# Experts' second layer: products of 256 columns in place of 512, in two passes over a token tile

## The chip, the core and the metric

The kernel runs on one core of one Trainium2 chip. Its engines work side by side and meet through semaphores: TensorE (PE in the profile, with its weight loads as PEld), VectorE (DVE), ScalarE (ACT), GpSimd (POOL) and SyncE (SP), which issues most of the transfers. The time is the device time of one execution in microseconds; before the change it was 1222.12 us, the median of three runs (1220.14 to 1223.38).

## What is computed

Three layers follow one another on 1152 tokens (2 x 576) of width 512, all in float32:

```
q_pool = q.reshape(B, H, S // 2, 2, D).mean(axis=3)                # attention on pooled queries
attn = softmax(scale * q_pool @ k^T);  x = attn @ v                # 2 x 8 heads, 1152 keys, width 64
h = x @ w_in;  x = (h * tanh(softplus(h))) @ w_out                 # 512 -> 2048 -> 512
P = exp(x @ w_gate - max), 8 rounds of row and column scaling       # the gate, 1152 x 8
for e in range(8):                                                  # experts, 512 -> 1024 -> 512
    h = np.maximum(x @ w1[e], 0.0)
    ye = h @ w2[e]
    out += P[:, e:e + 1] * ye
```

The change lies in `h @ w2[e]`, the experts' second layer.

## The kernel before

To keep float32 accuracy, every operand of a large product is split into a high and a low part of type fp32r, and a product is made as three: high weight x low data and the like (names end in h and l). Each product loads 128 x 128 values as weights and streams the other operand past them, up to 512 columns, into a bank of PSUM (128 x 512 float32 values). Eight banks are shared by the pools `ps_o` (three) and `ps_h` (five).

The experts are cut along their hidden width of 8 x 1024 into 64 chunks of 128. The first four chunks go ahead (called the shared layer here, group -1 in the code); the other 60 form 20 groups of three (`groups`, line 958). A group is worked off in two stages:

- first layer (`product`, line 1081): 15 block products in a scheme that saves products by adding blocks, each of 6 products of 384 columns, 90 in all. DVE and ACT combine the banks and write the hidden values, split, to `hhall` and `hlall`;
- second layer (`down`, line 1234): for each of the nine token tiles of 128 tokens, three chunks x three operand pairs, 9 products of 512 columns into one bank `po`; the hidden values are the weights of a product, the expert's matrix `wdb` streams past. When the last product is done, DVE multiplies the bank by the gate and adds it to `oacc` in one instruction (line 1259). Where a group crosses from one expert to the next (5 of 20 groups), a tile has two banks, one for each expert, and two such instructions (`segments`, line 961). The shared layer has 12 products a tile, and ACT copies the bank (line 1255).

In the last group the last tile of `TILES` (tile 3) is already made in two halves: `parts` is 2, and each half of 256 columns has a bank, an addition and an output transfer of its own.

The order of the work is written out by hand: each engine runs its instructions in the order in which the loops at lines 1289 to 1317 issue them. Between two tiles of the second layer `next_weights` prepares the next group's weights on DVE, ACT and POOL (`w_sum`, `w_split`, `down_split`). In the shared layer, group 0 and at the start of group 1, the gate's rounds are put between the tiles (`gate_step`): each is a small product on PE (`psk`, line 913), which reads `csum`, and a short chain on DVE that ends with the reduction to the next `csum` (lines 903 to 918).

Of the kernel before, what the change touches and what calls it, by code (L numbers as in the profile page):

```python
# [23 lines left out]
def pool_attention_mish_sinkhorn_kernel(  # L24
# [12 lines left out]
    nc = tc.nc  # L37
# [263 lines left out]
    with ExitStack() as actx:  # L301
# [234 lines left out]
        c0, c1 = 2 * P, SQ  # L536
# [264 lines left out]
    def hidden(c, a, b):  # L801
        return tuple((y if c == NFC - 1 else x[:, c, :])[:, a:b] for x, y in hall)
# [43 lines left out]
    while len(todo) > NDC or k < NB:  # L846
# [3 lines left out]
        while len(todo) > NDC and todo[0][0] <= k and room >= todo[0][1]:  # L850
            _, n, s, th, dc = todo.pop(0)
# [109 lines left out]
    def segments(g):  # L961

        if g < 0:
            return [(0, list(range(NFC)))]
        es = [c // NHC for c in groups[g]]
        return [(e, [j for j in range(CH) if es[j] == e]) for e in sorted(set(es))]
# [253 lines left out]
    def token_rows(t):  # L1220

        cuts = sorted({0, P} | {x - t * P for b in range(B) for x in range(b * SQ, (b + 1) * SQ + 1, P)
                                if 0 < x - t * P < P} | {x * SQ - t * P for x in range(B) if 0 < x * SQ - t * P < P})
        for a, z in zip(cuts, cuts[1:]):
            b, i = divmod(t * P + a, SQ)
            if i < MID * P:
                r = b * SQ + i % P * MID + i // P
                yield slice(a, z), slice(r, r + (z - a - 1) * MID + 1, MID)
            else:
                yield slice(a, z), slice(b * SQ + i, b * SQ + i + z - a)  # L1230
# [3 lines left out]
    def down(g, t):  # L1234

        end = g == NG - 1
        parts = 2 if end and t == TILES[-1] else 1
        w = DM // parts
        for si, (e, sl) in enumerate(segments(g)):
            gate = Pm[:, t, e:e + 1]  # L1240
            for j in range(parts):
                pl, tag = (ps_h, "h") if (3 <= t < 8 if g < 0 else si) else (ps_o, "o")
                ps = pl.tile([P, 512], F32, tag=tag, name=f"po{g}_{t}_{e}_{j}")
                cs = slice(j * w, (j + 1) * w)
                ops = []
                for c in sl:
                    hh, hl = hidden(c, t * P, (t + 1) * P)
                    whi, wlo = wdt[g, c]
                    ops += [(hh, wlo), (hl, whi), (hh, whi)]
                for n, (a, b) in enumerate(ops):  # L1250
                    nc.tensor.matmul(  # L1251
                        ps[:, 0:w], lhsT=a, rhs=b[:, cs], start=(n == 0), stop=(n == len(ops) - 1))
                oa = oacc[:, t, cs]
                if g < 0:
                    nc.scalar.activation(oa, ps[:, 0:w], AF.Copy)
                elif g == 0:
                    nc.vector.tensor_tensor(out=oa, in0=ps[:, 0:w], in1=oa, op=ALU.add)
                else:
                    nc.vector.scalar_tensor_tensor(  # L1259
                        out=oa, in0=ps[:, 0:w], scalar=gate, in1=oa, op0=ALU.mult, op1=ALU.add)  # L1260
                if end and e == segments(g)[-1][0]:
                    for rows, to in token_rows(t):
                        nc.sync.dma_start(out=out[to, cs], in_=oa[rows])
# [25 lines left out]
    for t in range(NTT):  # L1289
        down(-1, t)  # L1290
        next_weights(0, t - 2)
        if t == 7:
            gate_step()

    spare += [hp_.tile([P, 3, TH], F32, tag="last" + x, name="spare" + x) for x in "hl"]
    for g in range(NG):
        for k, n in enumerate(ORDER3):
            product(g, n)
            after(g, n)
            if k + NSL < NP:  # L1300
                w_split(g, k + NSL)
            if k in ((0, 7, 9) if g == 0 else (7, 9)):
                down_split(g, {0: 0, 7: 1, 9: 2}[k])
            if k == 9 and g + 1 < NG:
                raw_up(g + 1)
            if (g, k) in ((0, 0), (1, 0)):
                gate_step()
            if g == 1 and k in (10, 12, 14):
                assert not gate_steps
                scale(k // 2 - 5)  # L1310
        for k, t in enumerate(TILES):
            down(g, t)
            next_weights(g + 1, k)
            if g == 0 and k in (1, 3, 4, 6, 7):
                gate_step()
            if g == 1 and k + 3 < NTT:
                scale(k + 3)
# [30 lines left out]
```

## Time and profile before

| what | us |
|---|---|
| median of three timed runs | 1222.12 |
| the profiled execution | 1218.55 |
| its span, first to last instruction | 1215.9 |
| PE busy | 1200.9 (99%) |
| weight loads busy | 1108.4 (91%) |
| DVE / POOL / ACT busy | 851.1 / 656.2 / 592.3 |

The profile is of one execution. Products on PE overlap in it: the duration of one is longer than the distance from its start to the next start, so a pace is read from starts or from the chain, not from durations. The chain of waits follows the work that ended last back from the end; consecutive products of one line are merged into one piece of it with their number. Times in a timeline are microseconds from the start of the span.

### The profile page before, as it was taken

To read this page: it belongs to the slowest core of one execution; us is meant where nothing else is said; L and a number is where in the kernel's file an instruction comes from. 1 tells how busy PE (TensorE), PEld (TensorE's weight loads), DVE (VectorE), ACT (ScalarE), POOL (GpSimd) and SP (SyncE) were. 2 spreads that over 40 slices of the span, in tenths; PEclk is the share of its full clock that TensorE was granted. 3 is DMA by queue.
4 is the path that set the end of the run, shared out by engine and by line. 5 is a ranking of instruction groups with operands and counts; after the bars stand their busy time and mean duration, and the time that the engine had idled before them with its cause. 6 is when DMAs were issued, how large, how long until landed. Compare 5 with 4: busy or idle time off the path is not lost.

```text
span 1215.9 us, 19367 instructions
## 1 busy us (share of the span) xinstructions
PE 1200.9 (99%) x6840; PEld 1108.4 (91%) x6840; DVE 851.1 (70%) x1576; ACT 592.3 (49%) x1357; POOL 656.2 (54%) x758
## 2 busy tenths in 40 slices
PE   8999999999999999999999999999999999999998
PEld 7999999999999999888988889999888889999887
DVE  7889999965444334787866678776866677766865
ACT  7889999976544443543333223333332233333331
POOL 7567877425443332475655556645545566555551
PEclk9999999999999999999999999999999999999999
DMA  6788888644232210011101111111111111111112
GB/s 193 256 274 278 282 283 282 230 145 139 70 93 82 70 44 18 1 53 53 53 23 39 52 53 45 52 53 53 33 38 44 53 44 53 53 52 42 33 40 78
DMA packets 51984, 116.38 MB, mean 96 GB/s; under 512 B 7977, under 2 KB 22897, under 8 KB 51889
## 3 DMA queue, kind: packets, MB, share of 16 engines
q1 hardware_dynamic: 48400, 103.36, 26.1%
q0 software_dynamic: 3488, 11.80, 3.6%
q8 instruction: 54, 0.88, 0.3%
q14 instruction: 42, 0.34, 0.1%
HBM read 66.86 MB, written 2.40 MB: 57 GB/s over the span
## 4 chain that ended last, share of the span: by engine, by line
PE 91%; DVE 4%; DMA 2%; issue 1%; ACT 1%; SPq 0%; POOL 0%; ACTq 0%
PE po L1251 30%; PE c L1081 26%; PE ph L234 10%; PE po L820 8%; PE psS L484 5%; PE psA L585 5%; PE psT L564 3%; DMA er<-e 2%; DVE e L489 2%; DVE etl L570 1%; PE psk L419 1%; ACT e L503 0%; DMA kraw<-in_k_dram 0%; PE pg L875 0%; PE psq L462 0%
## 5 line engine op out<-in xcount | busy, mean ns | idle before, releaser
L82 POOL TENSOR_TENSOR wslotsl<-s,wslotsh 128x256 fp32r<-128x256 f32 x180 | 131.5, 739 | 238.0 <-ACT wslotsh L75 238.0
L1259 DVE SCALAR_TENSOR_TENSOR oacc<-po,Pm,oacc 128x512 f32<-128x512 f32 (+1 forms) x217 | 161.1, 746 | 102.4 <-PE po L1251 95.9
L1251 PE MATMUL po<-wdbl,hhall 128*128 128x512 f32 (+1 forms) x543 | 214.4, 395 | 0.0
L1251 PE MATMUL po<-wdbh,hlall 128*128 128x512 f32 (+1 forms) x543 | 214.1, 394 | 0.0
L1251 PE MATMUL po<-wdbh,hhall 128*128 128x512 f32 (+1 forms) x543 | 214.0, 394 | 0.0
L1098 ACT ACTIVATE t<-c 128x384 f32<-128x384 f32 x80 | 39.2, 489 | 247.3 <-PE c L1081 247.3
L1118 ACT ACTIVATE hhall<-c 128x384 fp32r<-128x384 f32 x180 | 88.5, 492 | 127.7 <-DVE c L1114 125.0
L1251 PEld LDWEIGHTS po<-wdbh,hhall 128*128 128x128 f32 x543 | 102.1, 188 | 24.3
L1251 PEld LDWEIGHTS po<-wdbl,hhall 128*128 128x128 f32 x543 | 102.1, 188 | 23.3
L1251 PEld LDWEIGHTS po<-wdbh,hlall 128*128 128x128 f32 x543 | 102.1, 188 | 23.2
L82 POOL TENSOR_TENSOR wslotsl<-rawu,wslotsh 128x256 fp32r<-128x256 f32 x120 | 91.0, 772 | 50.2 <-ACT wslotsh L75 50.2
L570 DVE TENSOR_TENSOR etl<-psT,eth 128x384 fp32r<-128x384 f32 (+1 forms) x240 | 108.2, 509 | 7.3 <-ACT eth L567 6.6
L489 DVE TENSOR_SCALAR_CACHE_REDUCE e<-psS 128x1152 f32<-128x1152 f32 x72 | 97.6, 1356 | 17.7 <-PE psS L484 13.8
L1119 DVE SCALAR_TENSOR_TENSOR hlall<-c,hhall 128x384 fp32r<-128x384 f32 x180 | 98.7, 548 | 2.0
L567 ACT ACTIVATE eth<-psT 128x384 fp32r<-128x384 f32 (+1 forms) x240 | 92.1, 472 | 6.9 <-PE psT L564 6.5
L1081 PE MATMUL c<-x2l,wslotsh 128*128 128x384 f32 x280 | 94.3, 337 | 0.0
L1081 PE MATMUL c<-x2h,wslotsl 128*128 128x384 f32 x280 | 94.2, 336 | 0.0
L1081 PE MATMUL c<-x2h,wslotsh 128*128 128x384 f32 x280 | 93.9, 335 | 0.0
L503 ACT ACTIVATE e<-e,nm 128x1152 f32<-128x1152 f32 x70 | 89.2, 1274 | 2.7 <-DVE e L489 1.8
L484 PE MATMUL psS<-kT,qT 128*128 128x384 f32 x384 | 81.9, 348 | 1.9 <-DVE e L489 1.5
L75 ACT ACTIVATE wslotsh<-s 128x256 fp32r<-128x256 f32 x180 | 72.0, 410 | 23.9 <-DVE s L1047 23.8
L585 PE MATMUL psA<-etl,vst 128*128 128x256 f32 (+1 forms) x288 | 81.2, 304 | 0.8 <-DVE rs L512 0.4
(368 smaller groups left out, 3065.0 us busy)
## 6 DMA issues: line engine op xcount, KB each, us to landing
er<-e SPq DMA_DIRECT2D x70, 576.0 KB, 4.1
rawd<-in_moe_w_dram SPq DMA_DIRECT2D x60, 256.0 KB, 2.8
rawu<-in_moe_w_dram SPq DMA_DIRECT2D x30, 384.0 KB, 3.3
raw<-in_moe_w_in_dram SPq DMA_DIRECT2D x16, 512.0 KB, 3.8
raw<-in_moe_w_out_dram SPq DMA_DIRECT2D x16, 512.0 KB, 3.7
vraw<-in_v_dram POOLq DMA_DIRECT2D x15, 288.0 KB, 4.3
kraw<-in_k_dram POOLq DMA_DIRECT2D x13, 288.0 KB, 4.1
qT<-qT SPq DMA_DIRECT2D x28, 128.0 KB, 4.8
```

The costliest lines, as they stand in the source:

```text
L82: eng.tensor_tensor(out=lo, in0=src, in1=hi.bitcast(F32), op=ALU.subtract)
L234: nc.tensor.matmul(ps[:, 0:TH], lhsT=a, rhs=b, start=(n == 0), stop=(n == len(ops) - 1))
L484: nc.tensor.matmul(ps[:, kb, 0:TH], lhsT=a, rhs=kt[:, kb * TH:(kb + 1) * TH], start=(n == 0), stop=(n == len(ops) - 1))
L489: nc.vector.tensor_scalar(sc, ps[:, :, 0:TH], -1.0, None, op0=ALU.mult, op1=ALU.min, accum_out=nm)
L567: nc.scalar.activation(eh[:, cs, o:o + b - a], ps[:, 0:3, a:b], AF.Copy)
L570: nc.vector.tensor_tensor(out=el[:, cs, o:o + b - a], in0=ps[:, 0:3, a:b], in1=eh[:, cs, o:o + b - a].bitcast(F32), op=ALU.subtract)
L585: nc.tensor.matmul(box["ps"][:, 0:n], lhsT=vst[p, j][:, c].rearrange("p a d -> p (a d)"), rhs=(el, eh)[which][:, c, 0:n], start=(c == 0 an ...
L820: nc.tensor.matmul(ps[:, 0:TH], lhsT=a, rhs=b, start=(n == 0), stop=(n == len(ops) - 1))
L1081: nc.tensor.matmul(cb[c], lhsT=a_, rhs=b_, start=FIRST[n] and m == 0, stop=LAST[n] and m == len(ops) - 1, skip_group_check=True)
L1119: los.append(lambda: nc.vector.scalar_tensor_tensor(out=lo, in0=b, scalar=0.0, in1=hi.bitcast(F32), op0=ALU.max, op1=ALU.subtract))
L1251: nc.tensor.matmul(ps[:, 0:w], lhsT=a, rhs=b[:, cs], start=(n == 0), stop=(n == len(ops) - 1))
L1259: nc.vector.scalar_tensor_tensor(out=oa, in0=ps[:, 0:w], scalar=gate, in1=oa, op0=ALU.mult, op1=ALU.add)
```

## The change

Only `down` changes. In place of one pass over the operand pairs with 512 columns, a loop over `c0` makes one whole pass for columns 0 to 255 and then one for 256 to 511. Both halves lie in the same bank; each begins its sum anew (`start`) and ends it (`stop`). So each weight block is loaded twice, once for each half. The tile's evacuation still reads the whole bank at once, after the second half. The last tile of the last group, with `w` = 256, is as before.

```diff
--- before.py
+++ after.py
@@ -1247,9 +1247,11 @@
                     hh, hl = hidden(c, t * P, (t + 1) * P)
                     whi, wlo = wdt[g, c]
                     ops += [(hh, wlo), (hl, whi), (hh, whi)]
-                for n, (a, b) in enumerate(ops):
-                    nc.tensor.matmul(
-                        ps[:, 0:w], lhsT=a, rhs=b[:, cs], start=(n == 0), stop=(n == len(ops) - 1))
+                for c0 in range(0, w, 256):
+                    for n, (a, b) in enumerate(ops):
+                        nc.tensor.matmul(
+                            ps[:, c0:c0 + 256], lhsT=a, rhs=b[:, cs.start + c0:cs.start + c0 + 256],
+                            start=(n == 0), stop=(n == len(ops) - 1))
                 oa = oacc[:, t, cs]
                 if g < 0:
                     nc.scalar.activation(oa, ps[:, 0:w], AF.Copy)
```

The order of the instructions on DVE, ACT, POOL and SP is the same in both kernels, with the same waits. On PE there are 1719 rows more. Two places show it. The first is a token tile of the last group (`po_5_7_0`: tile 5, expert 7), with the row ahead of it and the first one of the last tile. Before:

```order
L1251 MATMUL po_4_7_0_12745<-wdbh,hhall 128x512
L1251 MATMUL po_5_7_0_12758<-wdbl,hhall 128x512 [waits DVE_49]
L1251 MATMUL po_5_7_0_12758<-wdbh,hlall 128x512
L1251 MATMUL po_5_7_0_12758<-wdbh,hhall 128x512
L1251 MATMUL po_5_7_0_12758<-wdbl,hhall 128x512
L1251 MATMUL po_5_7_0_12758<-wdbh,hlall 128x512
L1251 MATMUL po_5_7_0_12758<-wdbh,hhall 128x512
L1251 MATMUL po_5_7_0_12758<-wdbl,hhall 128x512
L1251 MATMUL po_5_7_0_12758<-wdbh,hlall 128x512
L1251 MATMUL po_5_7_0_12758<-wdbh,hhall 128x512
L1251 MATMUL po_3_7_0_12771<-wdbl,hhall 128x256 [waits DVE_49]
```

And with the change, from the last row of the tile's first half on:

```order
L1252 MATMUL po_5_7_0_14468<-wdbh,hhall 128x256
L1252 MATMUL po_5_7_0_14468<-wdbl,hhall 128x256
L1252 MATMUL po_5_7_0_14468<-wdbh,hlall 128x256
L1252 MATMUL po_5_7_0_14468<-wdbh,hhall 128x256
L1252 MATMUL po_5_7_0_14468<-wdbl,hhall 128x256
L1252 MATMUL po_5_7_0_14468<-wdbh,hlall 128x256
L1252 MATMUL po_5_7_0_14468<-wdbh,hhall 128x256
L1252 MATMUL po_5_7_0_14468<-wdbl,hhall 128x256
L1252 MATMUL po_5_7_0_14468<-wdbh,hlall 128x256
L1252 MATMUL po_5_7_0_14468<-wdbh,hhall 128x256
L1252 MATMUL po_3_7_0_14490<-wdbl,hhall 128x256 [waits DVE_49]
```

The nine rows of a tile are eighteen now, the three operand pairs of the three chunks once for each half; the wait for a free bank stands at the first row of the tile alone, and the last tile (`po_3_7_0`) is as it was.

The second place is the end of the shared layer on PE: the last products of its tile 8 (`po-1_8`), the first block product of group 0 (`c`) and the gate product that follows (`psk`). Before:

```order
L1251 MATMUL po-1_8_0_0_6513<-wdh_5835,hllast 128x512
L1251 MATMUL po-1_8_0_0_6513<-wdh_5835,hhlast 128x512
L1081 MATMUL c_0_6531<-x2h,wslotsl 128x384 [waits Pool_49]
L1081 MATMUL c_0_6531<-x2l,wslotsh 128x384 [waits Activation_49]
L1081 MATMUL c_0_6531<-x2h,wslotsh 128x384
L1081 MATMUL c_0_6531<-x2h,wslotsl 128x384
L1081 MATMUL c_0_6531<-x2l,wslotsh 128x384
L1081 MATMUL c_0_6531<-x2h,wslotsh 128x384
L913 MATMUL psk_6546<-csum,ones 128x8 [waits DVE_49]
L1081 MATMUL c_0_6554<-x2h,wslotsl 128x384 [waits Pool_49]
```

With the change:

```order
L1252 MATMUL po-1_8_0_0_6609<-wdh_5835,hllast 128x256
L1252 MATMUL po-1_8_0_0_6609<-wdh_5835,hhlast 128x256
L1081 MATMUL c_0_6639<-x2h,wslotsl 128x384 [waits Pool_49]
L1081 MATMUL c_0_6639<-x2l,wslotsh 128x384 [waits Activation_49]
L1081 MATMUL c_0_6639<-x2h,wslotsh 128x384
L1081 MATMUL c_0_6639<-x2h,wslotsl 128x384
L1081 MATMUL c_0_6639<-x2l,wslotsh 128x384
L1081 MATMUL c_0_6639<-x2h,wslotsh 128x384
L913 MATMUL psk_6654<-csum,ones 128x8 [waits DVE_49]
L1081 MATMUL c_0_6662<-x2h,wslotsl 128x384 [waits PE_49,Pool_49]
```

The gate product stands behind the same six products of `c` as before and waits for DVE as before; 108 more products stand ahead of it since the shared layer began. The product of `c` behind it has one more wait, for PE itself. Such a wait is new at eight places, all in the shared layer, group 0 and the first products of group 1: here, at the first product of five tiles of group 0 and of tile 0 of the shared layer, and at products of `c` or `psk`.

## Rows read from the trace of the kernel before

**Rows 1.** Page: busy time of PE; shares of the chain by engine and by line.

```profile
PE 1200.9 (99%) x6840; PEld 1108.4 (91%) x6840; DVE 851.1 (70%) x1576; ACT 592.3 (49%) x1357; POOL 656.2 (54%) x758
...
PE 91%; DVE 4%; DMA 2%; issue 1%; ACT 1%; SPq 0%; POOL 0%; ACTq 0%
PE po L1251 30%; PE c L1081 26%; PE ph L234 10%; PE po L820 8%; PE psS L484 5%; PE psA L585 5%; PE psT L564 3%; DMA er<-e 2%; DVE e L489 2%; DVE etl L570 1%; PE psk L419 1%; ACT e L503 0%; DMA kraw<-in_k_dram 0%; PE pg L875 0%; PE psq L462 
```

**Rows 2.** Chain in order of time: start us, us, what; a group in mid-kernel.

```profile
1124.39 18.90 PE po L1251 x81
1143.29 15.65 PE c L1081 x90
```

**Rows 3.** Groups of line 1251 by form; then the timeline of PE at the end.

```profile
L1251 PE MATMUL po<-wdbl,hhall 128*128 128x512 f32 x537 | 212.7, 396 | 0.0
L1251 PE MATMUL po<-wdbl,hhall 128*128 128x256 f32 x6 | 1.7, 277 | 0.0
L1251 PEld LDWEIGHTS po<-wdbh,hlall 128*128 128x128 f32 x543 | 102.1, 188 | 23.2
...
1209.88 0.40 PE L1251 MATMUL po<-wdbh,hhall 128*128 128x512 f32 x1
1210.12 0.28 PE L1251 MATMUL po<-wdbl,hhall 128*128 128x256 f32 x1
1210.12 0.19 PEld L1251 LDWEIGHTS po<-wdbh,hlall 128*128 128x128 f32 x1
1210.24 0.28 PE L1251 MATMUL po<-wdbh,hlall 128*128 128x256 f32 x1
...
1212.05 0.28 PE L1251 MATMUL po<-wdbh,hhall 128*128 128x256 f32 x1
```

**Rows 4.** Timeline of PE in the attention stage, line 585.

```profile
262.97 0.33 PE L234 MATMUL ph<-xl,wuh 128*128 128x384 f32 x1
263.14 0.33 PE L234 MATMUL ph<-xh,wuh 128*128 128x384 f32 x1
263.31 0.28 PE L585 MATMUL psA<-etl,vst 128*128 128x256 f32 x1
...
265.34 0.28 PE L585 MATMUL psA<-eth,vst 128*128 128x256 f32 x1
```

**Rows 5.** Busy time by stretch: attention, a crossing group's second layer, another group's.

```profile
core 0: us, PE busy (x) PEld busy (x) DVE busy (x) ACT busy (x) POOL busy (x), PEclk, DMA share, GB/s
188.00:206.90 18.90, 18.85 (x151) 18.63 (x152) 16.68 (x34) 17.42 (x39) 15.99 (x18) 1.00 0.85 293
744.30:763.20 18.90, 18.90 (x83) 15.28 (x82) 17.81 (x29) 3.52 (x10) 9.38 (x12) 1.00 0.10 34
778.90:797.80 18.90, 18.90 (x83) 15.23 (x83) 12.14 (x20) 3.42 (x10) 9.60 (x12) 1.00 0.12 40
```

**Rows 6.** Timeline of DVE, then PE, at the gate product; chain, shared layer and group 0.

```profile
514.38 0.94 DVE L1047 TENSOR_TENSOR rawu<-rawu 128x256 f32<-128x256 f32 x1 [0.64 <-POOL s L1047]
...
518.32 0.30 DVE L907 TENSOR_REDUCE csum<-Pm 128x8 f32<-128x80 f32 x1
...
518.68 0.39 PE L913 MATMUL psk<-csum,ones 128*128 128x8 f32 x2
...
492.34 2.80 PE po-1_0_0_0_6354 L1251 x12
...
533.79 4.21 PE po L1251 x18
...
546.40 4.31 PE po L1251 x18
...
553.71 2.20 PE po L1251 x9
```

**Rows 7.** Timeline of DVE at the end of the crossing group's second layer.

```profile
761.38 3.11 DVE L1259 SCALAR_TENSOR_TENSOR oacc<-po,Pm,oacc 128x512 f32<-128x512 f32 x4
766.05 0.57 DVE L1114 TENSOR_TENSOR c<-c,t 128x384 f32<-128x384 f32 x1 [1.56 <-ACT t L1098]
```

## The prediction, made before the changed kernel was run

> **What bounds the kernel now.** I read the busy table first [rows 1]: the tensor engine (PE) has a product in flight for 99% of the span of 1215.9 us, and the chain that ended last lies on it for 91%; line 1251, the second layer, is the largest piece with 30%. The chain in order of time [rows 2] shows the steady state that the change touches: 81 products of line 1251 for 18.90 us, 90 products of line 1081 for 15.65 us; this pair repeats from 571.81 us to the end without a step of another engine between. So inside 19 of the 20 groups nothing but PE's own pace sets the time, and a faster or slower product goes straight into the end. Only around 515 to 556 us do steps of VectorE (DVE) stand between [rows 6]. The granted clock is 1.00 in every stage I read [rows 5], which is the upper of its two levels (2.4 GHz), so no part of the pace comes from the clock.
>
> The pace by width, start to start, is what counts, since the durations of products overlap. 512 columns: 18.90 us / 81 = 233.3 ns. 384 columns: 15.65 / 90 = 173.9 ns [rows 2]. 256 columns: the trace has them twice. At the very end, the last token tile is already made in two halves of 256, with the same line and tiles [rows 3]: the first starts at 1210.12, the last of the 18 at 1212.05, so 1.93 us / 17 steps = 113.5 ns; without the first step, which follows a product of 512, 1.81 / 16 = 113.1. I take 113.4. The step from the first half to the second (10th product) shows no gap. In the attention stage the value product (line 585) also has 256 columns: 263.31 to 265.34, 2.03 us / 17 = 119.4 ns [rows 4].
>
> **The change, part by part.** It removes 1719 products of 512 columns: 537 of each of three operand pairs, 1611 [rows 3], and 108 of the shared layer (nine tiles of 12 [rows 6]). It adds 3438 of 256 with as many weight loads. Evacuations, splits, weight DMAs and the order on DVE, ScalarE (ACT), GpSimd (POOL) and SyncE stay as they are, so the whole sum is PE's pace and what covers it.
>
> - *Price of a pair.* By the nearest row, line 1251 itself at 256, two halves cost 2 x 113.4 = 226.8 ns against 233.3: 6.5 ns less. The printed starts have 0.01 us, so a pace from 16 or 17 steps is good to 0.6 ns, the pair to 1.2: 5.3 to 7.7 saved. By the farther row, line 585, a pair costs 2 x 119.4 = 238.8: 5.5 ns more. These are both ends. I take the first: same line, same weight and hidden tiles, same slices of the moving operand. The three paces also lie on one line: 113.4, 173.9, 233.3 rise by 60.5 and 59.4 for each 128 columns, and carried down to no columns that leaves about -6 ns; a product pays no fixed piece that halving would pay twice.
> - *Weight loads.* Twice as many, each 188 ns long in the trace [rows 3], but they overlap with products: in the end stretch each load starts with the product before it and the pace stays 113. Their price is thus inside the 113.4. Whether pairs of load and product can be issued that fast for long is bounded by the attention stage: 151 products with 152 loads in 18.9 us [rows 5], 8.0 per us with its waits included; the changed stage needs 1/0.1134 = 8.8 per us.
> - *Waits of PE on itself.* Eight products (in the shared layer, group 0 and what directly follows) now also wait for an earlier PE product. Those should be on banks written tiles ago, so I cost them at nothing. Were one to wait for the product just before it, it would cost at most the duration less the pace, 277 - 113 = 164 ns [rows 3]; eight of them 1.3 us.
> - *Where the gain reaches the end.* Groups 1 to 19: 18 x 81 + 72 products (the last tile is halved already) = 1530, x 6.5 = 9.95 us. Cover: DVE must still empty the banks. In five groups a chunk boundary between experts makes two sums per tile, and DVE is busy 17.81 of 18.90 us [rows 5]; the stage would become 81 x 0.2268 = 18.37 us, so DVE still fits, and after it DVE has 1.56 us idle before its next step [rows 7], against 0.53 us that PE comes earlier. If that cover failed, it costs at most 5 x 0.53 = 2.6 us.
> - *Shared layer.* 108 x 6.5 = 0.70 us earlier, and lost again. The second gate product (psk, line 913) starts at 518.68 behind a DVE reduction that ends at 518.32 + 0.30 = 518.62 [rows 6]. PE would come there at about 517.95 and wait. That reduction doesn't move: DVE comes to it over eight rows without a break from 514.38 on, and the first of these waited for a POOL sum, not for PE's second layer. I count 0 for these 108.
> - *Group 0.* The chain there goes PE x18, DVE, PE x18, DVE, PE x9 [rows 6]: only 45 of its 81 products are on the path, 45 x 6.5 = 0.29 us; 36 are hidden behind the gate's DVE steps.
>
> Sum: 9.95 + 0 + 0.29 = 10.2 us. The profiled execution took 1218.55 us (span 1215.9 and 2.65 around it); it would take 1208.3. It was 3.6 us under the median of the three timed runs, 1222.12, from which I subtract the same: **1211.9 us**. With 5.3 and 7.7 ns on 1575 products the gain is 8.3 to 12.1 us, so 1210 to 1213.8.
>
> **The rivals.**
>
> *R1, the middle pace is 119, not 113 (slower).* The end stretch is quiet: ACT and POOL have finished. If, with other engines reading and writing, halves run as line 585 does, a pair costs 5.5 ns more: x 1719 = 9.5 us, 1231.6. It decides at 116.7 ns a half. For it: line 585 is the only row of 256 columns among busy engines, 17 steps alike. Against it: products of 384 directly before that stretch start 0.17 us apart (262.97, 263.14, 263.31) [rows 4], the pace that they have elsewhere, so the load of other engines isn't seen in the neighbours; and line 585 reads other tiles, with another row pitch.
>
> *R2, a fixed piece per product.* If a half pays a small piece of its own that the short end stretch hides, the pair lies between no gain and R1; at the middle, 2.75 ns over 233.3, x 1719 = 4.7 us: 1226.8. Against it is the line through the three widths. The Trainium skill states such a rule: "TensorE: Matmul & The Clock Gate", section "Back-to-back issue gap", has a warm gap of columns / 2.4 plus about 2.5 ns. By it a split would add 2.5 ns a pair, 4.3 us in all, an estimate from that page. The trace doesn't agree: it would be 215.8 for 512 and 109.2 for 256, and the rows have 233.3 and 113.4.
>
> *R3, the gain is covered elsewhere.* DVE in the five crossing groups (2.6 us) and PE's waits on itself (1.3 us) eat 3.9 us: 1215.8. Still faster. For it: the 94% DVE share in those groups; against it: DVE's idle time right after.
>
> *R4, nothing changes.* Two halves cost what the whole did, 1222. This needs the end stretch to be wrong by 3.3 ns a half, five times its reading error. That the change would not do what it says is out: the changed order of PE has 1719 more products.
>
> **How the numbers follow.** Forecast 0.74, R3 0.08, R1 0.10, R2 0.05, R4 0.03. A measurement of this kernel tells about 0.3%, 3.7 us, from no change. Faster: forecast and R3, 0.82. Same: R4 and the near part of R2, 0.05. Slower: R1 and most of R2, 0.13. The runs shown differ by 3.2 us, so I widen the forecast's 1210 to 1213.8 by 2 us down, and up to 1218 to take in R3: 1208 to 1218 leaves out R1, R2 and R4, under 2 in 10.
>
> **What would show it.** In the changed profile: 162 products of line 1252 (as line 1251 is then) in about 18.37 us in a steady group, the period of two stages 34.0 us in place of 34.55, starts 113 ns apart while DVE and POOL work; line 1081 unchanged at 15.65; a new wait of some 0.7 us of psk on the DVE reduction after the shared layer. Starts of 117 ns or more in mid-kernel make the forecast wrong, as do waits of PE on DVE in the crossing groups, or gaps between the two halves of a tile.

## The result, and the profile after

The changed kernel takes 1209.3 us, the median of five runs (1207.9 to 1209.99); before took 1222.12 on the same chip (five runs, 1218.86 to 1223.38). The ratio is 0.9905, with a 95% interval of 0.9888 to 0.9922: 9.5 to 13.7 us less. The forecast was 1211.9, with a range of 1208 to 1218.

The page of the changed kernel, its busy table and the groups of the changed line (name, form, count, then busy us and mean ns of one):

```profile
span 1207.9 us, 22808 instructions
...
PE 1192.0 (99%) x8559; PEld 1177.6 (97%) x8559; DVE 856.8 (71%) x1576; ACT 592.5 (49%) x1357; POOL 656.2 (54%) x758
...
L1252 PE MATMUL po<-wdbl,hhall 128*128 128x256 f32 x1080 | 298.6, 277 | 0.0
...
L1252 PEld LDWEIGHTS po<-wdbl,hhall 128*128 128x128 f32 x1080 | 202.8, 188 | 0.0
```

Beside [rows 1, 3]: 1719 products more, on PE alone, and the weight loads are now in flight for 97% of the span in place of 91%. The busy time of line 1252 must not be read as dearer: a product of 256 columns is in flight for 277 ns, but the next starts long before that. What counts is the stage, which the chain in order of time shows for a pair of stages in mid-kernel and for the last group:

```profile
743.82 18.36 PE po L1252 x162
762.18 15.66 PE c L1081 x90
777.84 18.36 PE po L1252 x162
...
1186.04 18.38 PE po L1252 x162
```

[Rows 2] had 18.90 and 15.65. The second layer's stage is 0.54 us shorter, the first layer's is where it was, and no step of another engine came between. Eighteen groups of 0.54 us and the last one (18.86 before, 18.38 now, since its last tile was halved already) make 10.2 us. The last group in the chain of before:

```profile
1193.48 18.86 PE po L1251 x90
```

The timeline of PE shows the pace, with the starts of one tile's first half and what follows:

```profile
777.67 0.28 PE L1252 MATMUL po<-wdbl,hhall 128*128 128x256 f32 x1
777.79 0.28 PE L1252 MATMUL po<-wdbh,hlall 128*128 128x256 f32 x1
...
778.58 0.28 PE L1252 MATMUL po<-wdbh,hhall 128*128 128x256 f32 x1
778.70 0.28 PE L1252 MATMUL po<-wdbl,hhall 128*128 128x256 f32 x1
...
780.17 0.28 PE L1252 MATMUL po<-wdbh,hlall 128*128 128x256 f32 x1
```

From 777.67 to 780.17 are 22 steps of 113.6 ns. The step from the first half to the second (778.58 to 778.70) is like the others, and so is that to the next tile.

The profiled runs differ by less than the medians: 1218.55 us before, 1209.99 after, 8.6 us. The part of the program that is the same in both explains it. The first product of the shared layer starts at 492.18 us before and at 494.88 after (the first row is from before, the second from after):

```profile
492.18 0.39 PE L1251 MATMUL po-1_0_0_0_6354<-wdl,hhall 128*128 128x512 f32 x1
...
494.88 0.28 PE L1252 MATMUL po-1_0_0_0_6354<-wdl,hhall 128*128 128x256 f32 x1
```

From there to the end of the span it is 723.7 us before and 713.0 after, 10.7 less. The experiments below, with nothing changed ahead of that product, had it between 492.23 and 495.30. A difference of spans thus holds some 3 us of chance from the first 492 us, and the stages are what to compare.

### The profile page after: what moved, and what is told of

It reads as the page before. It is cut to its first block, busy times and chain, and to the rows that moved or that the text cites. A ratio compares the mean times of both kernels' runs of the same rounds, so it can differ in the third digit from the quotient of the medians.

```text
span 1207.9 us, 22808 instructions
## 1 busy us (share of the span) xinstructions
PE 1192.0 (99%) x8559; PEld 1177.6 (97%) x8559; DVE 856.8 (71%) x1576; ACT 592.5 (49%) x1357; POOL 656.2 (54%) x758
## 4 chain that ended last, share of the span: by engine, by line
PE 54%; DVE 1%; issue 0%
PE po L1252 29%; PE c L1081 25%; DVE s L1047 0%; DVE oacc L1259 0%; DVE Pm L905 0%; DVE Pm L915 0%; DVE csum L907 0%; PE psk L913 0%; DVE rawu L1047 0%; DVE rsum L903 0%; DVE rsum L904 0%; DVE oacc L1261 0%; DVE crec L914 0%
## 5 line engine op out<-in xcount | busy, mean ns | idle before, releaser
L1252 PE MATMUL po<-wdbl,hhall 128*128 128x256 f32 x1080 | 298.6, 277 | 0.0
L1252 PE MATMUL po<-wdbh,hhall 128*128 128x256 f32 x1080 | 298.2, 276 | 0.0
L1252 PE MATMUL po<-wdbh,hlall 128*128 128x256 f32 x1080 | 298.2, 276 | 0.0
L1252 PEld LDWEIGHTS po<-wdbl,hhall 128*128 128x128 f32 x1080 | 202.8, 188 | 0.0
L1252 PEld LDWEIGHTS po<-wdbh,hhall 128*128 128x128 f32 x1080 | 202.8, 188 | 0.0
L1252 PEld LDWEIGHTS po<-wdbh,hlall 128*128 128x128 f32 x1080 | 202.8, 188 | 0.0
```

What stands on the lines that cost most here:

```text
L1252: nc.tensor.matmul(ps[:, c0:c0 + 256], lhsT=a, rhs=b[:, cs.start + c0:cs.start + c0 + 256], start=(n == 0), stop=(n == len(ops) - 1))
```

## The experiments

Edits are shown against the changed kernel, without the lines that stay; where an edit names `c1`, the line of the product takes the columns from `c0` to `c1` too. The first four ran together on one chip beside eight runs of the kernel before (median 1218.55 us), the next three beside ten (1219.91), the last beside one (1219.66).

**Quarters: how far does narrowing go on paying?**

```diff
-                for c0 in range(0, w, 256):
+                for c0 in range(0, w, 128):
-                            ps[:, c0:c0 + 256], lhsT=a, rhs=b[:, cs.start + c0:cs.start + c0 + 256],
+                            ps[:, c0:c0 + 128], lhsT=a, rhs=b[:, cs.start + c0:cs.start + c0 + 128],
```

> A tile's products in four passes of 128 columns (6876 products in place of 1719). Theory A (the price is the columns': 60 ns for each 128 of them less a piece of about 6.5 ns, weight loads hidden at any width): 53 ns a quarter, 4 x 53 = 213 ns against 226.7 for two halves, 1719 x 13.5 = 23 us faster than the changed kernel, about 1186 us. Theory B (at 256 columns the weight load sets the pace already, since each load starts with the product before it): quarters at 113 ns too, 453 ns, 1719 x 226 = 389 us slower, about 1600 us. Theory C (a weight load takes as long as the transposes' pace of 84 to 88 ns in the trace before): 4 x 86 = 344, 1719 x 117 = 202 us slower, about 1411 us.

One run, 1585.44 us: 376 us more than with halves. The chain has the stage at 36.13 us for 324 products, 111.5 ns each; a half costs 113.4:

```profile
1492.15 36.13 PE po L1252 x324
```

The timeline of PE and of the weight loads in that kernel:

```profile
900.01 0.19 PEld L1252 LDWEIGHTS po<-wdbl,hhall 128*128 128x128 f32 x1
900.07 0.27 PE L1252 MATMUL po<-wdbl,hhall 128*128 128x128 f32 x1
900.12 0.19 PEld L1252 LDWEIGHTS po<-wdbh,hlall 128*128 128x128 f32 x1
900.18 0.27 PE L1252 MATMUL po<-wdbh,hlall 128*128 128x128 f32 x1
```

The loads follow each other at 0.11 us and each product comes 0.06 us after its load has started. With halves it is the other way round, as the prediction's [rows 3] show: a load starts when the product before it does (both at 1210.12), and the products set the step. So below some width the time is not that of the columns but, in this stage, a floor of 111.5 ns for each load with its product. That is theory B; the straight line of the prediction would have given 53 ns for 128 columns, and it is wrong below 256. Theory C fell here, but the transposes that it was taken from do run faster, in the kernel before:

```profile
182.14 0.93 PE L564 MATMUL psT<-identr,er 128*128 128x128 f32 x9
182.90 0.35 PE L585 MATMUL psA<-eth,vst 128*128 128x256 f32 x1
```

Nine transposes of 128 columns, with a load each, take 0.76 us to the next start, 84 ns apiece; their loads are in flight for 140 ns, those of the second layer for 188. So 111.5 ns is a floor of these products, not of every load with its product. What makes the difference wasn't tried.

**An uneven cut, 192 and 320: is the floor the same for another width, and what does 320 cost?**

```diff
-                for c0 in range(0, w, 256):
+                for c0, c1 in ((0, 192), (192, 512)) if w == 512 else ((0, 256),):
```

> A tile's products in two passes of 192 and 320 columns. Theory A (a straight line in the columns, loads hidden): 83.3 + 143.3 = 226.7 ns, as with two halves, 1209 us. Theory A2 (a step for each begun block of 128 columns: 320 columns cost 146.7 as line 585 does in the trace before, 192 then 86.7): 233.3, the gain is gone, about 1221 us. Theory B (weight loads need 113 ns): 113 + 146.7 = 260, 1719 x 33 = 57 us over the changed kernel, about 1266 us. Theory C (loads need 86 ns): 86 + 146.7 = 233, about 1220 us.

1261.23 us, ratio 1.0349 (1.0310 to 1.0388). The timeline of PE:

```profile
1240.32 0.28 PE L1252 MATMUL po<-wdbh,hhall 128*128 128x192 f32 x1
...
1240.99 0.27 PE L1252 MATMUL po<-wdbh,hhall 128*128 128x192 f32 x1
1241.10 0.33 PE L1252 MATMUL po<-wdbl,hhall 128*128 128x320 f32 x1
1241.27 0.31 PE L1252 MATMUL po<-wdbh,hlall 128*128 128x320 f32 x1
...
1241.86 0.31 PE L1252 MATMUL po<-wdbh,hhall 128*128 128x320 f32 x1
```

192 columns take 0.67 us / 6 = 112 ns, the pace of 128; 320 take 0.59 / 4 = 147. A steady group in the chain:

```profile
1199.06 20.91 PE po L1252 x162
```

The sum of columns is that of two halves, the pair costs 258.1 ns (20.91 us / 81) in place of 226.7: theory B again, which had 260. The floor is the same for 128 and 192 columns, and what a part held at it loses is more than the cut can gain.

**The halves in turn: is it the width, or the order?**

```diff
-                for c0 in range(0, w, 256):
-                    for n, (a, b) in enumerate(ops):
+                for n, (a, b) in enumerate(ops):
+                    for c0 in range(0, w, 256):
-                            start=(n == 0), stop=(n == len(ops) - 1))
+                            start=(n == 0 and c0 == 0), stop=(n == len(ops) - 1), skip_group_check=True)
```

> The two halves take turns for each operand pair, in place of one whole pass after the other; the number of products and loads, the widths and the waits are those of the changed kernel. If the gain comes from the width of a product alone (theory A or B): a pace of 113 ns and about 1209 us, 0.99 of before. If it needs a run of products on the same 256 columns of a bank (rival): the pair goes back to 233 ns, about 1221 us.

1209.24 us, ratio 0.9924 (0.9900 to 0.9947), the same as in two passes; the stage of a steady group in the chain is 18.36 us for 162 products. Here the same weights are loaded twice in a row and consecutive products write different halves of the bank. Neither matters to the pace. It is the width.

**The kernel before, once more: how much do two profiles of one kernel differ?** No edit.

> The kernel before, once more, for the spread between executions: 1218 to 1224 us. The first product of the shared layer started at 492.2 us in the profile before and at 494.9 in the one after, though nothing ahead of it was changed. If that is spread between executions, this profile may lie anywhere from 491 to 496 us; if the changed program delays its own start, it lies at 492 again. The gate product after the shared layer comes 26.5 us after the shared layer's first product, as in the profile before, or up to 0.7 us sooner if a stretched step on DVE there (0.84 us in one profile, 0.23 in the other) is chance.

One run, 1221.36 us. The shared layer starts at 494.52 us in place of 492.18, and the stage of a steady group is 18.90 us again. Two profiles of one kernel differ by 2.3 us before the first changed product, and by nothing in the stages.

**The expert's matrix at another address: is that why line 585 has 119 ns?**

```diff
-                    pool.tile([P, 4, GF], F32R, tag=nm + x, name=f"{nm}{x}{i}") for x in "hl")
+                    pool.tile([P, 4 * GF + 64 * which], F32R, tag=nm + x, name=f"{nm}{x}{i}")[:, 0:4 * GF].rearrange(
+                        "p (a f) -> p a f", a=4) for x in "hl")
-            wdt["all"] = tuple(wpools["d0"].tile([P, 4, GF], F32R, tag="wd" + x, name=f"wdb{x}") for x in "hl")
+            wdt["all"] = tuple(wpools["d0"].tile([P, 4 * GF + 64], F32R, tag="wd" + x, name=f"wdb{x}")[:, 64:].rearrange(
+                "p (a f) -> p a f", a=4) for x in "hl")
```

> The changed kernel with the low and high blocks of the second layer's weights laid out anew, so that in two of three operand pairs (those with wdbh) the streamed rows begin 256 bytes further along; wdbl keeps its place within 512 bytes and is the control. If line 585's pace of 119 ns for 256 columns comes from where its rows begin in memory (the reason that the prediction gave beside R1): 119 to 120 ns after products with wdbh, 113 with wdbl, 2292 x 6.5 = 15 us over the changed kernel, about 1224 us. If not: 113 throughout and about 1209 us, and line 585's pace has another cause.

1208.72 us, ratio 0.9902 (0.9871 to 0.9933): no difference to the changed kernel. By the sizes in the edit, the high part's start moved by 256 bytes within 512 and the low part's did not. The timeline of PE, 15 steps in 1.70 us, 113.3 ns:

```profile
1189.79 0.28 PE L1254 MATMUL po<-wdbl,hhall 128*128 128x256 f32 x1
...
1191.49 0.28 PE L1254 MATMUL po<-wdbl,hhall 128*128 128x256 f32 x1
```

The three operand pairs keep one pace at both places. That idea fell, and what gives line 585 its 119 ns stays open.

**264 and 248: a straight line or a stair?**

```diff
-                for c0 in range(0, w, 256):
+                for c0, c1 in ((0, 264), (264, 512)) if w == 512 else ((0, 256),):
```

> A tile's products in two passes of 264 and 248 columns. Stair (columns at 2.4 GHz, 0.417 ns each, and 6.7 ns for each further begun block of 128: fits 320, 384 and 512 columns at 146.7, 173.3 and 233.3): 264 columns cost 110 + 13.3 = 123.3 ns, 248 cost 110, or what a load needs, 111.5: 234.8 a pair, 1719 x 8.1 = 14 us over the changed kernel, about 1223 us. Line (0.469 ns a column less 6.7 ns, as the prediction had it): 117.1 and 111.5 (the load's pace; 109.6 by the columns), 228.6 a pair, about 1212 us. Start to start of the 264 decides: 123 or 117 ns.

1228.84 us, ratio 1.0075 (1.0045 to 1.0104). The timeline of PE:

```profile
1171.92 0.28 PE L1252 MATMUL po<-wdbl,hhall 128*128 128x248 f32 x1
...
1172.85 0.28 PE L1252 MATMUL po<-wdbh,hhall 128*128 128x248 f32 x1
...
1173.09 0.29 PE L1252 MATMUL po<-wdbh,hlall 128*128 128x264 f32 x1
...
1173.96 0.28 PE L1252 MATMUL po<-wdbh,hhall 128*128 128x264 f32 x1
```

264 columns take 0.87 us / 7 = 124 ns: eight columns more than 256 cost 11 ns, where the straight line had 3.7. The stair had 123.3. But 248 take 0.93 / 8 = 116 ns, more than 256 and more than either theory's 111.5. Those 4 to 5 ns go the same way as the 6 us by which the kernel lies over the stair's 1223. The stair holds at the widths tried from 256 up; what happens just under it isn't explained by it.

**Halves in the shared layer alone: what of that layer's gain is kept?**

```diff
-                for c0 in range(0, w, 256):
+                wide = 256 if g < 0 else w
+                for c0 in range(0, w, wide):
-                            ps[:, c0:c0 + 256], lhsT=a, rhs=b[:, cs.start + c0:cs.start + c0 + 256],
+                            ps[:, c0:c0 + wide], lhsT=a, rhs=b[:, cs.start + c0:cs.start + c0 + wide],
```

> Halves of 256 columns in the shared layer alone (108 products), 512 elsewhere. The prediction: the layer itself ends 0.7 us sooner, and the second gate product does not come sooner, 26.5 us after the layer's first product, because DVE's reduction before it does not move; the kernel takes 1217 to 1223 us like before. The other view, from the profile after (25.87 us, with a step of DVE at line 905 of 0.23 us where it was 0.84): the gate product comes 0.6 us sooner whenever that step is not stretched, which has nothing to do with PE.

One run, 1220.65 us, and 18.90 us for a steady stage. The first block product of group 0 comes 24.73 us after the layer's first product, 0.68 less than before (25.41). The second gate product comes 25.90 us after it, where before has 26.50. The timeline of DVE, PE and POOL at that place, in this kernel:

```profile
520.49 0.23 DVE L905 TENSOR_TENSOR Pm<-Pm,rsum 128x72 f32<-128x72 f32 x1
520.50 1.70 POOL L82 TENSOR_TENSOR wslotsl<-s,wslotsh 128x256 fp32r<-128x256 f32 x2
...
520.76 0.30 DVE L907 TENSOR_REDUCE csum<-Pm 128x8 f32<-128x80 f32 x1
521.12 0.39 PE L913 MATMUL psk<-csum,ones 128*128 128x8 f32 x2
```

And with the halves in turn, where PE has the wait that the prediction named:

```profile
517.51 0.82 DVE L905 TENSOR_TENSOR Pm<-Pm,rsum 128x72 f32<-128x72 f32 x1
517.51 1.42 POOL L82 TENSOR_TENSOR wslotsl<-s,wslotsh 128x256 fp32r<-128x256 f32 x2
...
518.37 0.30 DVE L907 TENSOR_REDUCE csum<-Pm 128x8 f32<-128x80 f32 x1
518.73 0.39 PE L913 MATMUL psk<-csum,ones 128*128 128x8 f32 x2 [0.55 <-DVE csum L907]
```

And in the kernel before:

```profile
517.45 0.84 DVE L905 TENSOR_TENSOR Pm<-Pm,rsum 128x72 f32<-128x72 f32 x1
```

The DVE product of line 905 takes 0.23 us in one and 0.82 in the other. Where it takes 0.82, nothing of the 0.68 is kept: the gate product comes 26.50 us after the layer's first, as before. Where it takes 0.23, 0.6 us are kept. Both profiles of the kernel before had 0.83 to 0.84; the changed kernel's own had 0.23, the shifted one, with the same products on PE, 0.83.

The traces show what goes with the stretch: a POOL product of line 82, a piece of the split of the next weights, which at this place starts within 0.02 us of the DVE step. Where the DVE step is long, it ends about 0.1 us after that POOL product does; where it is short, the two POOL products of the fences above take 1.70 us in place of 1.42. Line 905 runs 80 times in the ten profiles. The 21 steps over 0.24 us, 0.38 to 0.85 us long, all overlap a POOL instruction, and no step that overlaps none is longer than 0.24. So one of the two engines waits for the other. The starts don't tell which: DVE's lies some 0.02 us ahead in the kernel before, where DVE waits, and in the changed kernel, where it doesn't. Whether the change has a part in it is therefore open, and no run took the POOL product away.

**The half in the middle of the bank: is a block of 128 counted from the bank's start, or from the product's own first column?**

```diff
-                for c0 in range(0, w, 256):
+                for c0, c1 in ((0, 64), (64, 320), (320, 512)) if w == 512 else ((0, 256),):
```

> A tile's products in three passes of 64, 256 and 192 columns, so that the 256 lie at columns 64 to 319 of the bank and pass its columns 128 and 256. By count (a product pays 6.7 ns for each further block of 128 of its own columns): the 256 keep 113.3 ns. By place (it pays where it passes a multiple of 128 in the bank or in the streamed row): two such places, 120 ns, the pace that line 585 has. The passes of 64 and 192 should run at the load's pace, 111 to 112 ns each, so the three cost 336 or 343 ns and the kernel takes about 1209 + 1719 x 0.110 = 1398 us by count, 1410 us by place.

One run, 1400.15 us. The timeline of PE:

```profile
1384.16 0.36 PE L1252 MATMUL po<-wdbl,hhall 128*128 128x256 f32 x1
1384.36 0.28 PE L1252 MATMUL po<-wdbh,hlall 128*128 128x256 f32 x1
1384.48 0.28 PE L1252 MATMUL po<-wdbh,hhall 128*128 128x256 f32 x1
...
1385.16 0.28 PE L1252 MATMUL po<-wdbh,hhall 128*128 128x256 f32 x1
1385.27 0.25 PE L1252 MATMUL po<-wdbl,hhall 128*128 128x192 f32 x1
1385.36 0.28 PE L1252 MATMUL po<-wdbh,hlall 128*128 128x192 f32 x1
...
1386.26 0.21 PE L1252 MATMUL po<-wdbl,hhall 128*128 128x64 f32 x1
1386.31 0.28 PE L1252 MATMUL po<-wdbh,hlall 128*128 128x64 f32 x1
1386.42 0.28 PE L1252 MATMUL po<-wdbh,hhall 128*128 128x64 f32 x1
```

256 columns across three of the bank's blocks take 0.68 us / 6 = 113.3 ns, as at the bank's start: counted by the product's own columns. 64 columns take 0.11 us, the floor again. The first product of 256 after the narrow ones takes 0.20 us, 0.09 over the pace, and most of it comes back in the same tile: the step after the first product of 192 is 0.09 us and that after the first of 64 is 0.05, in place of 0.11. It is a shift of the starts more than a cost.

## Why the prediction was right, and where its reason was not

**The price of a pair** was 6.5 ns less; it is 0.54 us / 81 = 6.7 ns. The place to read it was the last tile of the kernel before [rows 3], and the pace of that quiet stretch holds among busy engines: 113.6 ns in mid-kernel against 113.4.

**The reason given for it was half right.** "A product pays no fixed piece that halving would pay twice" is true, but not because time is a straight line through 113.4, 173.9 and 233.3. The runs show a stair and a floor. What fits the five widths measured from 256 up is 0.417 ns a column (what one column a cycle would be at the upper level, 2.4 GHz) plus about 6.7 ns for each further begun block of 128 columns of the product:

| columns | 0.417 ns each | further blocks x 6.7 | sum | measured |
|---|---|---|---|---|
| 256 | 106.7 | 1 | 113.3 | 113.6 |
| 264 | 110.0 | 2 | 123.3 | 124 |
| 320 | 133.3 | 2 | 146.7 | 147 |
| 384 | 160.0 | 2 | 173.3 | 173.9 |
| 512 | 213.3 | 3 | 233.3 | 233.3 |

By this fit one product of 512 pays three such pieces, two halves pay two; the change saves the one between them. The widths of 64, 128 and 192 columns run at the floor, 111 to 112 ns. 256 lies 2 ns above it, and of the cuts tried only the halves gain. The line predicted the same price since all three of its points are multiples of 128 above the floor. Had the change cut into quarters, the same reasoning would have promised 23 us more and lost 376 against the halves. What the 6.7 ns are isn't shown; the stair is a description, and only its step just above 256 was measured on both sides (256 and 264). It misses 248 columns (110 by the stair, 111.5 by the floor, 116 measured).

**Weight loads** were called hidden inside the 113.4. They are, but barely: 111.5 of 113.4 ns. The prediction's bound on their rate, 8.0 a microsecond in the attention stage, lay under the 8.8 that the change needs and so settled nothing; what settled it was the 18 products of the last tile. The floor itself, 9.0, could be read from no row of before, where the transposes make 11.9. That the floor is the load's pace is read from where the loads start; the load wasn't measured without its product. The Trainium skill, "TensorE: Matmul & The Clock Gate", section "LDWEIGHTS (loading the stationary operand)", has a load last its columns over 1.2, which would make 107 ns for 128, an estimate. The floor measured here is 4 to 5% above that; the 84 ns of the transposes lie under it.

**Rivals.** R1, a mid-kernel pace of 119, fell with the first stage in the chain. Its ground, line 585, keeps its 119 ns unexplained, so the choice between the two rows was right by nearness, and not because the cause of the difference was known. The argument of the other tiles and their layout, which the prediction used against R1, found no support when the address was moved (the row pitch was not tried apart). R2, a fixed piece per product, fell too: the pair is 6.7 ns cheaper. By the Trainium skill's rule that the prediction quoted with it ("TensorE: Matmul & The Clock Gate", section "Back-to-back issue gap") it would be 2.5 ns dearer, an estimate. R4 would have needed 233.3 ns a pair.

**DVE in the crossing groups (R3)** has room. The windows of the crossing group's second layer and of another's (us, then busy PE, PEld, DVE, ACT, POOL, clock, DMA share, GB/s), and the end of the former on DVE:

```profile
745.20:763.60 18.40, 18.40 (x160) 18.40 (x160) 17.33 (x27) 2.81 (x9) 9.38 (x12) 1.00 0.05 17
777.84:796.20 18.36, 18.36 (x163) 18.36 (x163) 12.44 (x20) 3.25 (x10) 9.54 (x12) 1.00 0.10 35
```

```profile
760.69 3.11 DVE L1261 SCALAR_TENSOR_TENSOR oacc<-po,Pm,oacc 128x512 f32<-128x512 f32 x4
764.83 0.57 DVE L1114 TENSOR_TENSOR c<-c,t 128x384 f32<-128x384 f32 x1 [1.03 <-ACT t L1098]
```

The idle time after the stage was 1.56 us [rows 7] and is 1.03: the 0.53 us by which PE comes earlier were taken out of it, as forecast, and PE didn't wait. The clock is 1.00 in both stages, as before [rows 5].

**The shared layer** was counted at 0, with 0.70 us gained and lost again at the gate product. It gained 0.68, and whether it is lost depends on the DVE step of line 905: all of it is when that step is stretched beside a POOL product, 0.6 us is kept when not. In the changed kernel's own profile it was kept, with a wait of 0.24 us:

```profile
520.12 0.23 DVE L905 TENSOR_TENSOR Pm<-Pm,rsum 128x72 f32<-128x72 f32 x1
520.39 0.30 DVE L907 TENSOR_REDUCE csum<-Pm 128x8 f32<-128x80 f32 x1
520.74 0.30 PEld L913 LDWEIGHTS psk<-csum,ones 128*128 128x128 f32 x2 [0.24 <-DVE csum L907]
```

"That reduction doesn't move" was wrong as a fixed time, since the step ahead of it hasn't one.

**Group 0** was to give 0.29 us. From its first second-layer product to its last gate product, two profiles of before have 23.17 and 23.88 us, and the run with halves in the shared layer alone, whose group 0 is as before, 23.17; that of the changed kernel has 23.01, that with halves in turn 22.90 and the shifted one 23.01. That is 0.16 to 0.27 less than 23.17, but the spread of before, 0.7 us, covers the term; it is neither shown nor refuted. **PE's waits on itself** cost nothing: no gap longer than those of before stands at these products.

**The sum.** Groups 1 to 19 give 10.2 us where 9.95 were forecast, the shared layer 0 to 0.6, group 0 an unknown few tenths: some 10.2 to 11 us. From the first product of the shared layer to the end of the span, the two profiles of before take 723.7 and 724.1 us; the changed kernel takes 713.0, the halves in turn 713.2 and the shifted one 713.8. That is 10 to 11 us less, as the stages say. The median fell by 12.8, the interval begins at 9.5. The rest isn't in any stage, and the 492 us ahead of the change vary by more than it; that the median came 2.6 us under the forecast is therefore no sign of another gain.

## What to carry to other kernels

Look for the price of a new shape in the kernel before: a tail, an edge tile or another layer often runs it already, and its start-to-start pace was worth more here than the line drawn through other widths. Take the nearest such row: the two rows of 256 columns, 113 and 119 ns, differed by enough to turn the sign of the forecast. A line through a few widths says nothing below the narrowest, and at 264 columns it was 7 ns off between them; ask which other instruction goes with each product, here the weight load, and where its pace takes over. And compare stages, not spans, when the gain is about 1% and the unchanged part of the program varies by 3 us.

## What the runs showed of the hardware that was not expected

- The second layer's products fit a step for each further begun 128 columns: 264 columns take 124 ns, 256 take 113.3. Products of 512 columns (233.3 ns) lose to two of 256 (226.7), though these load the weights twice.
- Their pace has a floor of 111.5 ns for a load and its product, at 64, 128 and 192 columns alike, though the transposes of line 564 run at 84 ns with a load each; 248 columns, at 116 ns, are dearer than 256.
- The first product of 256 columns after a stretch at the floor takes 200 ns, the next ones 113 to 118; the first narrow ones after it take 90 and 50, so most of it comes back.
- One small DVE product (128 x 72) takes 0.23 us alone and up to 0.85 beside a POOL product; where it stays short beside one, the POOL products are the longer ones (two take 1.70 us in place of 1.42).
